# First MLP layer, second product: the low weights of the last F tile multiply all 128 rows

## The chip, the cores and the metric

The program runs on one core of one Trainium2 chip. The metric is device time in microseconds (us), over several executions. The engines are named as in the profile: PE (TensorE, the matmuls), PEld (its weight loads), DVE (VectorE), ACT (ScalarE), POOL (GpSimd), SP (SyncE, which issues most DMAs).

## The reference

Four layers over x of 2048 tokens by 640 channels: a spectral filter, a token MLP, and both again, with residuals. The change lies in the first MLP, whose hidden size F is 1728:

```python
def _B_ref(x, w1, b1, w2, b2):
    h = _layernorm(x, axis=-1)                       # (B, S, D)
    u = jnp.einsum("bsd,sf->bdf", h, w1) + b1        # (B, D, F)
    u = _gelu(u)
    y = jnp.einsum("bdf,fs->bds", u, w2) + b2        # (B, D, S)
    return y.transpose(0, 2, 1)

x = A_x
x = x + _A_ref(_layernorm(x, axis=-1), A_w_r, A_w_i)
x = x + _B_ref(_layernorm(x, axis=-1), B_w1, B_b1, B_w2, B_b2)
x = x + _A_ref(_layernorm(x, axis=-1), A_w_r, A_w_i)
x = x + _B_ref(_layernorm(x, axis=-1), B_w1, B_b1, B_w2, B_b2)
```

## The kernel before

Products in float32 precision are made of 16-bit parts: an operand is split into a high part and a low part (the rest), and three matmuls accumulate high by high, high by low and low by high (`mm3`, line 253). Stationary operands are weights; the moving operand has 320 columns, half of the 640 channels.

The first MLP is `b1st` (line 869). F is cut into 14 tiles of 128 rows (`NFT`). 13 of them are full; the last has 64 rows of its own, and the host lays these 64 out twice, so that rows 64 to 127 of the tile's weights repeat rows 0 to 63. The first product makes u tile by tile. `usplit` (line 918) then splits u: `uh` is the high part, `ul` the low part, one pair of tiles for each F tile. In the last F tile (13) `uh` is written on all 128 rows, then the lower part goes into rows 64 to 127 of `ul`, and rows 0 to 63 of `ul` take a copy of `uh` (lines 919 to 923). Since the weights are there twice, one matmul of the high weights `wh` with this `ul` gives high by high and high by low together. What is left for tile 13 is the low weights `wl` by the high part of u, over the 64 rows 0 to 63.

The second product (loop at line 1033) makes 16 output tiles j of 128 tokens. For each j it runs over the 14 F tiles and, in each, over the halves a = 0 and 1: three matmuls for F tiles 0 to 12 (line 1072), and two for tile 13 (lines 1074 and 1075). Two halves of tile 13 in each of 16 outputs make 32 matmuls of line 1075. In the last j (`tail`) the loop is sorted so that half 0 is done whole before half 1, and the next layer's first transform follows on its tail. Around the matmuls the same loop loads, scans and splits the weights of later outputs (`ahead`, `prep`, `step`), evicts the sum of the output with the bias and the residual x (line 1082), stores it, normalizes the row and folds it for the next layer (line 1086), and, two outputs later, multiplies it by that layer's first table (`flush`, the matmuls written `ps<-tM` in the profile).

PE works its instructions in program order. PSUM tiles come from a ring of four (`big`, line 88). Except in the tail the order on each engine is the order in which a scheduling layer issued the instructions. The helper `Pin` records every operation, so nearly all rows of the profile carry line 48; they are told apart by the names of their tiles.

Of the kernel before, what the change touches and what calls it, by code (L numbers as in the profile page):

```python
# [55 lines left out]
class Layers:  # L56
# [812 lines left out]
    def b1st(self, li):  # L869
        nc, A = self.nc, self.A  # L870
        V, G, T = self.V, self.G, self.T
        mm = self.PE.matmul
# [20 lines left out]
        uh = [pu.tile([128, 2, 320], F16, name=f"uh{f}_{self.n}") for f in range(NFT)]  # L893
# [7 lines left out]
        def ahead(m):  # L901

            if m + 3 < NFT + NJ:
                self.wload(m + 3)
            if m + 1 < NFT + NJ:
                self.wopen(m + 1)

        def prep(m):

            for c in range(2 if m + 1 < NFT + NJ else 0):  # L910
                self.wsplit(m + 1, (c,))
                yield

        def step(m):
            if m in sc:
                next(sc[m])

        def usplit(ft, t):
            V.tensor_scalar(uh[ft], t, self.su, None, op0=ALU.mult)
            c = slice(0 if ft < NFT - 1 else 64, 128)  # L920
            V.scalar_tensor_tensor(ul[ft][c], t[c], self.su[c], uh[ft][c], op0=ALU.mult, op1=ALU.subtract)
            if ft == NFT - 1:
                V.tensor_copy(ul[ft][:64], uh[ft][:64])

        def prod(ps, w, j, h, start=False, stop=False):
            for a in range(2):
                mm(ps[:, a, :320], w[:, j], h[:, a], start=start, stop=stop)
# [20 lines left out]
        for ft in range(NFT):  # L948
# [9 lines left out]
            for j in run:  # L958
                if ft == 0:
                    if j in (6, 7):  # L960
                        step(2)
                elif ft == 1:
                    if j in (1, 2):
                        next(steps)
                    if j in (8, 10):
                        self.scan1(3, (j // 2 - 4,))
                    if j == 15:
                        step(3)
                else:
                    if ft == 2 and j in (4, 5):  # L970
                        step(3)
                    if ft == 2 and j in (5, 6):
                        self.scan1(4, (j - 5,))
                    if ft == 2 and j == 7:
                        step(4)
                    if j in ((6, 8) if ft == 2 else (2, 4)):
                        next(steps)
                    if ft == 2 and j in (10, 11) or ft > 2 and j in (4, 5):
                        step(ft + 2)
                    if j == 8 and ft == NFT - 3:  # L980
                        self.scale_u()
                    if j in (11, 13):
                        self.scan1(ft + 3, (j // 2 - 5,))
                    if j == 15:
                        step(ft + 3)
                    if ft == NFT - 1 and 6 <= j:
                        usplit(j - 6, uf[j - 6])
# [16 lines left out]
        for k in range(10, NFT):  # L1004
            usplit(k, uf[k])
# [11 lines left out]
        def load(j):  # L1017
            if j < NJ - 1:
                xt = self.t(p, [128, D], F32, "xt", 3)
            else:  # L1020
                xt = self.t(p, [128, 642], F32, "zt", 1)
                G.memset(xt[:, D:], 0.0)
            nc.sync.dma_start(xt[:, :D], self.xs[li][j])
            return xt
# [4 lines left out]
        def flush(k):  # L1029
            while len(pend) > k:  # L1030
                self.s1_all(*pend.pop(0))

        for j in range(NJ):
            wh, wl = self.w.pop(NFT + j)
            ahead(NFT + j)
            m = NFT + j
            steps = prep(m)
            c2 = self.ct[1][:, j:j + 1]
            if j + 2 < NJ:
                xts.append(load(j + 2))  # L1040
            xt = xts[j][:, :D]
            T.activation(xt, xt, AF.Identity, bias=self.b2[:, j:j + 1])
            x2 = xt.rearrange("p (a b) -> p a b", a=2)
            tail = j == NJ - 1
            ps = self.big()
            pss = (ps[:, 0], self.big()[:, 0] if tail else ps[:, 1])
            order = [(ft, a) for ft in range(NFT) for a in range(2)]
            if tail:

                order.sort(key=lambda q: q[1])  # L1050
                st = self.t(p, [128, 2, 6], F32, "st", 2)
                self.pin = True

            def half(a):
                V.scalar_tensor_tensor(x2[:, a], pss[a][:, :320], c2, x2[:, a], op0=ALU.mult, op1=ALU.add)
                V.bn_stats(st[:, a], x2[:, a])

            for i, (ft, a) in enumerate(order):
                if tail and i == NFT:
                    half(0)  # L1060
                    flush(1)
                if i in (4, 8):
                    next(steps, None)
                if i in (6, 7):
                    step(m + 2)
                if i in (15, 18):
                    self.scan1(m + 3, (i // 3 - 5,))
                if i == 26 and m + 3 < NFT + NJ:
                    step(m + 3)
                o = pss[a][:, :320]  # L1070
                if ft < NFT - 1:
                    self.mm3(o, (wh[:, ft], wl[:, ft]), (uh[ft][:, a], ul[ft][:, a]), ft == 0, False)
                else:
                    mm(o, wh[:, ft], ul[ft][:, a], start=False, stop=False)
                    mm(o, wl[:64, ft], uh[ft][:64, a], start=False, stop=True)
            if tail:
                half(1)
                nc.sync.dma_start(self.xs[li + 1][j], xt)
                self.a0_tail(j, xts[j], st, pend)
                self.pin = False  # L1080
                break
            V.scalar_tensor_tensor(x2, ps[:, :, :320], c2, x2, op0=ALU.mult, op1=ALU.add)
            nc.sync.dma_start(self.xs[li + 1][j], xt)
            flush(1)
            r, b = self.stats_r(p, *self.stats(p, xt, self.CA, self.CB))
            pend.append((j, *self.a0_lo(*self.a0_hi(self.a0_fold2(self.a0_fold1(self.a0_norm(xt, r, b)))))))
# [616 lines left out]
```

## Time and profile before

| | |
|---|---|
| median of 3 runs | 1053.35 us (1052.02 to 1053.73) |
| span of the profiled execution, first to last instruction | 1049.4 us |
| median less that span | 3.9 us |
| mean granted TensorE clock | 0.976 |
| second product of the first MLP | 371.25 to 568.30 us |
| PE busy from 371.25 to 568.00 | 196.75 of 196.75 us |
| PEld, DVE, ACT, POOL busy in that stretch | 138.73, 120.58, 100.43, 38.72 us |
| DMA, mean share of 16 engines there | 0.39 |

The profile gives one execution; its own total beside the span is not recorded, so the span is compared with the median of the runs. PE and PEld are two rows of the same engine: a weight load can run while the matmul ahead of it runs. A matmul's recorded length (0.30 us) is longer than the step from one matmul to the next, since matmuls are pipelined; what a matmul costs in a full queue is read from the start of one to the start of the next. In matmul rows "128\*128" is contraction rows by output rows, and in "128x320" 320 is the moving columns.

### The profile page before, as it was taken

The numbers are of one execution on the slowest core, as the hardware profiler recorded it, in microseconds if no ns is written. First come the engines' busy times: TensorE is split into PE (matmuls) and PEld (weight loads), VectorE is DVE, ScalarE is ACT, GpSimd is POOL, SyncE is SP. The second block draws the span as 40 slices with busy tenths as digits, with TensorE's granted clock in tenths as the row PEclk, the third lists the DMA queues.
The fourth block names the chain that finished last, engine by engine and source line by source line (L and its number), as shares of the span: only waits on it lengthen the run. The fifth ranks groups of instructions, "written<-read, shape, count | busy, mean of one in ns | idle before, by whom it ended". The sixth has DMA issues, their size and how long they took to land.

```text
span 1049.4 us, 21203 instructions
## 1 busy us (share of the span) xinstructions
PE 1005.2 (96%) x8379; PEld 765.3 (73%) x8379; DVE 750.6 (72%) x1465; ACT 587.2 (56%) x904; POOL 289.2 (28%) x487
## 2 busy tenths in 40 slices
PE   4889898999999999999998998999999999999998
PEld 3768798777777776777775887986777777777776
DVE  7978979954333955666655797997655564987885
ACT  5858668776554555555532575784644454644532
POOL 6938877400000002111121587870000000000000
PEclk8599989999999999999999998999999999999999
DMA  7766355532222264434321652554422233445511
GB/s 230 267 190 201 94 176 198 176 114 89 83 81 78 74 236 152 122 121 134 121 78 55 207 164 98 191 184 165 143 98 82 74 106 94 138 139 178 166 43 51
DMA packets 55739, 141.48 MB, mean 135 GB/s; under 512 B 6460, under 2 KB 12248, under 8 KB 55384
## 3 DMA queue, kind: packets, MB, share of 16 engines
q1 hardware_dynamic: 54200, 131.97, 38.8%
q0 software_dynamic: 1440, 8.15, 2.5%
q8 instruction: 66, 1.08, 0.4%
q14 instruction: 33, 0.27, 0.1%
HBM read 117.03 MB, written 23.07 MB: 134 GB/s over the span
## 4 chain that ended last, share of the span: by engine, by line
PE 78%; DVE 15%; POOL 2%; issue 2%; ACT 1%; DMA 1%; SPq 0%; POOLq 0%; ACTq 0%; DVEq 0%
PE ps L48 78%; DVE xt L48 4%; DVE st L48 2%; DVE el L48 2%; DVE f L48 2%; DVE s1l L48 1%; DVE hl L48 1%; POOL ta L48 1%; DVE xl L48 1%; POOL eo L48 1%; DMA xt<-x 1%; DVE wl L48 0%; DVE ta L48 0%; DVE tb L48 0%; DMA raw<-w 0%
## 5 line engine op out<-in xcount | busy, mean ns | idle before, releaser
L48 PEld LDWEIGHTS <-wh 128*128 128x128 f16 x2992 | 289.5, 98 | 115.0 <-issue 0.8
L48 PEld LDWEIGHTS <-wl 128*128 128x128 f16 (+1 forms) x1616 | 157.8, 98 | 67.8 <-issue 4.5
L48 PE MATMUL ps<-hh,wh 128*128 128x320 f16 x896 | 186.0, 299 | 1.1 <-ACT hh L48 0.6
L48 PE MATMUL ps<-hl,wh 128*128 128x320 f16 x896 | 184.8, 299 | 0.0
L48 PE MATMUL ps<-hh,wl 128*128 128x320 f16 x832 | 171.5, 299 | 0.6 <-DVE wl L48 0.6
L48 DVE SCALAR_TENSOR_TENSOR wl<-raw,s,wh 128x1024 f16<-128x1024 f32 (+2 forms) x88 | 103.6, 1181 | 86.7 <-ACT wh L48 86.7
L48 PE MATMUL ps<-uh,wl 128*128 128x320 f16 x448 | 134.3, 300 | 0.0
L48 PE MATMUL ps<-ul,wh 128*128 128x320 f16 x448 | 133.7, 299 | 0.0
L48 ACT ACTIVATE wh<-raw,s 128x1024 f16<-128x1024 f32 (+2 forms) x92 | 94.8, 1048 | 69.3 <-PE ps L48 63.6
L48 POOL TENSOR_TENSOR r<-v,mh 128x1 f32<-128x1 f32 x64 | 35.5, 555 | 330.4 <-DVE nm L48 323.0
L48 PE MATMUL ps<-uh,wh 128*128 128x320 f16 x416 | 124.4, 299 | 0.0
L48 ACT ACTIVATE junk<-raw 128x896 bf16<-128x896 f32 (+1 forms) x60 | 59.6, 994 | 45.6 <-DMA raw<-w 45.3
L48 PE MATMUL ps<-u,wo 128*128 128x320 f16 x504 | 69.9, 299 | 0.0
L48 DVE TENSOR_TENSOR f<-eo 128x256 f32<-128x256 f32 (+1 forms) x124 | 39.0, 368 | 41.8 <-POOL eo L48 41.2
L48 PEld LDWEIGHTS <-wo 128*128 128x128 f16 x504 | 49.3, 98 | 19.1
L48 PE MATMUL ps<-tDi,yh 128*128 128x322 f32 x256 | 60.2, 322 | 1.2 <-ACT yh L48 1.2
L48 DVE BATCH_NORM_STATS2 st<-xt 128x6 f32<-128x320 f32 x126 | 55.3, 481 | 4.9 <-DMA xt<-x 4.8
L48 ACT ACTIVATE z<-xt,nb,r 128x640 f32<-128x640 f32 x31 | 28.5, 919 | 53.4 <-POOL z L48 42.9
L48 POOL TENSOR_TENSOR eo<-z 128x320 f32<-128x320 f32 x62 | 53.2, 880 | 17.0 <-ACT z L48 15.1
L48 PE MATMUL ps<-ph,tS 128*128 128x321 f16 (+2 forms) x288 | 57.9, 286 | 0.0
L48 PE MATMUL ps<-tM,f 128*128 128x128 f32 x160 | 38.3, 408 | 20.2 <-DMA xt<-x 11.7
L48 PEld LDWEIGHTS ps<-tM,f 128*128 128x128 f32 x160 | 32.3, 290 | 26.1 <-DVE f L48 25.5
(184 smaller groups left out, 2057.2 us busy)
## 6 DMA issues: line engine op xcount, KB each, us to landing
raw<-w SPq DMA_DIRECT2D x56, 512.0 KB
xt<-x SPq DMA_DIRECT2D x79, 320.0 KB
w<-w SPq DMA_DIRECT2D x48, 321.0 KB
x<-xt SPq DMA_DIRECT2D x47, 320.0 KB
raw<-w SPq DMA_DIRECT2D x32, 448.0 KB
raw<-w2z SPq DMA_DIRECT2D x32, 448.0 KB
out<-xt SPq DMA_DIRECT2D x15, 320.0 KB
tIM<-tIM POOLq DMA_DIRECT2D x8, 512.0 KB, 4.8
```

The lines of the kernel that those rows point to most:

```text
L48: i = f(*a, **k)
```

## The change

Two edits in `b1st`. After tile 13 of u is split, POOL writes zeros into rows 64 to 127 of its high part. And the 32 matmuls of the low weights of tile 13 take all 128 rows of the weights and of u instead of rows 0 to 63. The other 64 rows add weights times zero.

```diff
@@ usplit
             V.scalar_tensor_tensor(ul[ft][c], t[c], self.su[c], uh[ft][c], op0=ALU.mult, op1=ALU.subtract)
             if ft == NFT - 1:
                 V.tensor_copy(ul[ft][:64], uh[ft][:64])
+                G.memset(uh[ft][64:], 0.0)
@@ second product, last F tile
                     mm(o, wh[:, ft], ul[ft][:, a], start=False, stop=False)
-                    mm(o, wl[:64, ft], uh[ft][:64, a], start=False, stop=True)
+                    mm(o, wl[:, ft], uh[ft][:, a], start=False, stop=True)
```

The order of the instructions on PE, DVE, ACT and SP stays as it was. POOL has one instruction more, between the last work of the stage ahead of the MLP and the two small zero fills that it issues early for the next layer (`z` and `zt`). Before:

```order
L48 TENSOR_TENSOR r_3324<-v_3320,mh 128x1 [waits DVE_49,Activation_49]
L48 MEMSET z_5410 128x2
L48 MEMSET zt_7343 128x2 [waits PE_49]
L48 TENSOR_TENSOR r_5406<-v_5402,mh 128x1 [waits DVE_49]
L48 TENSOR_TENSOR nb_5408<-nm_5404,r_5406 128x1 [waits DVE_49,Pool_49]
```

With the change, where `uh_610_3417` is tile 13 of the high part and its wait on DVE is for the subtraction that reads these rows:

```order
L48 TENSOR_TENSOR r_3324<-v_3320,mh 128x1 [waits DVE_49,Activation_49]
L48 MEMSET uh_610_3417 64x640 [waits DVE_49,Activation_49,Pool_49]
L48 MEMSET z_5411 128x2 [waits Pool_49]
L48 MEMSET zt_7344 128x2 [waits PE_49]
L48 TENSOR_TENSOR r_5407<-v_5403,mh 128x1 [waits DVE_49]
```

The two small fills now stand behind the fill of `uh`, and the first `r` of the output loop behind these.

On PE, at the end of output j = 0, the rows with the change are these (`wh_5129` and `wl_5130` are the weights of j = 0):

```order
L48 MATMUL ps_5294<-ul_610_3431,wh_5129 128x320 [waits DVE_49]
L48 LDWEIGHTS wl_5130
L48 MATMUL ps_5294<-uh_610_3417,wl_5130 128x320 [waits Pool_49]
L48 LDWEIGHTS wh_5129
L48 MATMUL ps_5294<-ul_610_3431,wh_5129 128x320
L48 LDWEIGHTS wl_5130
L48 MATMUL ps_5294<-uh_610_3417,wl_5130 128x320
```

Before, the same seven rows stood there without the wait on POOL; no later matmul of the loop has gained a wait.

## The prediction

> **What bounds the kernel now.** I read the chain of waits first, then the stage that the change touches, then its matmuls one by one. From the page, the chain that ended last, and the chain cut to the stage:
>
> ```profile
> PE 78%; DVE 15%; POOL 2%; issue 2%; ACT 1%; DMA 1%; SPq 0%; POOLq 0%; ACTq 0%; DVEq 0%
> 359.97 208.33 PE ps L48 x1621
> 568.33 0.56 DVE zt L48
> 571.71 0.73 ACT fht L48
> ```
>
> From 359.97 to 568.3 us the chain never leaves PE. Nothing that another engine does in the second product (371.25 to 568.3) sets the end; what PE saves there, the end saves, until something else becomes late. Behind the product comes a serial tail of DVE and ACT that starts when the last matmul has ended, and so moves with it.
>
> The timeline of PE where output j = 0 passes to j = 1 (start us, length, out<-in, contraction rows by output rows, shape):
>
> ```profile
> 381.32 0.30 PE L48 MATMUL ps<-uh,wl 128*128 128x320 f16 x1
> 381.46 0.30 PE L48 MATMUL ps<-uh,wh 128*128 128x320 f16 x1
> 381.59 0.30 PE L48 MATMUL ps<-ul,wh 128*128 128x320 f16 x1
> 381.73 0.30 PE L48 MATMUL ps<-uh,wl 128*128 128x320 f16 x1
> 381.87 0.30 PE L48 MATMUL ps<-ul,wh 128*128 128x320 f16 x1
> 382.10 0.31 PE L48 MATMUL ps<-uh,wl 64*128 64x320 f16 x1
> 382.33 0.31 PE L48 MATMUL ps<-ul,wh 128*128 128x320 f16 x1
> 382.58 0.31 PE L48 MATMUL ps<-uh,wl 64*128 64x320 f16 x1
> 382.82 0.31 PE L48 MATMUL ps<-uh,wh 128*128 128x320 f16 x1
> ```
>
> The lengths are all alike and PE counts as busy throughout; the starts tell the cost. Four steps among matmuls of 128 rows, 381.32 to 381.87, take 0.55 us, 0.14 each. The four steps into and out of the two matmuls of 64 rows, 381.87 to 382.82, take 0.95 us. The weight loads of the same place say why:
>
> ```profile
> 381.73 0.10 PEld L48 LDWEIGHTS <-wh 128*128 128x128 f16 x1
> 382.09 0.09 PEld L48 LDWEIGHTS <-wl 64*128 64x128 f16 x1 [0.27 <-issue]
> 382.33 0.10 PEld L48 LDWEIGHTS <-wh 128*128 128x128 f16 x1
> 382.57 0.09 PEld L48 LDWEIGHTS <-wl 64*128 64x128 f16 x1
> ```
>
> Among 128-row matmuls a load runs one matmul ahead: the `wh` load of 381.73 ends before the `wh` matmul of 381.87 begins, while the one ahead of it runs. The 64-row load at 382.09 starts only with its own matmul (382.10), after 0.27 us in which the loader waited for nothing that the profile shows, and the 128-row load at 382.33 again only with its own. At each change of height the run-ahead is lost.
>
> Is it the change of height, or the height? Two other places tell:
>
> ```profile
> 582.96 0.23 PE L48 MATMUL ps<-tD,s1l 128*128 128x160 f16 x1
> 583.03 0.23 PE L48 MATMUL ps<-tD,stk 96*128 96x160 f16 x1
> 583.10 0.31 PE L48 MATMUL ps<-tD,s1h 128*128 128x161 f16 x2
> 610.34 0.28 PE L48 MATMUL ps<-tI,xh 64*128 64x128 f16 x4
> 610.51 0.28 PE L48 MATMUL ps<-tI,xh 64*128 64x128 f16 x4
> 610.62 0.22 PE L48 MATMUL ps<-tI,xl 64*128 64x128 f16 x2
> 610.77 0.31 PE L48 MATMUL ps<-ph,tS 128*128 128x321 f16 x1
> ```
>
> A 96-row matmul between 128-row ones steps by 0.07 us on both sides, the same as its neighbours of 160 columns, so fewer rows alone cost nothing. 64-row matmuls among themselves are quick (four of `xh` and two of `xl` between 610.34 and 610.51, 0.03 us each), but the last two and the way out to 128 rows take 0.15 us. The price is on the border between 64 and 128 rows.
>
> **The change, part by part.** The same 32 matmuls with the same 320 columns stay; their count and that of their loads do not change:
>
> ```profile
> L48 PE MATMUL ps<-uh,wl 128*128 128x320 f16 x416 | 124.4, 299 | 0.0
> L48 PE MATMUL ps<-uh,wl 64*128 64x320 f16 x32 | 9.8, 307 | 0.0
> L48 PEld LDWEIGHTS <-wl 64*128 64x128 f16 x32 | 3.0, 93 | 6.7 <-issue 4.5
> 567.75 0.30 PE L48 MATMUL ps<-ul,wh 128*128 128x320 f16 x1
> 567.99 0.31 PE L48 MATMUL ps<-uh,wl 64*128 64x320 f16 x1
> 568.23 0.28 PE L48 MATMUL ps<-tM,fh 128*128 128x128 f16 x2
> ```
>
> Term 1, the borders. Each output has four, and they cost 0.95 - 0.55 = 0.40 us more than four plain steps. The last ones, 0.24 us each at 567.75 to 568.23, cost the same as the first. 16 outputs: 16 x 0.40 = 6.4 us. The very last way out lies behind the matmul that DVE waits for, and PE then stands idle anyhow, so 0.24 - 0.14 = 0.1 us is not gained: 6.3 us. After the change the `uh,wl` matmuls of tile 13 have the form of the 416 others, all steps of which are plain, so I take the whole of it. The 6.7 us that the loader waited ahead of these 32 loads, 0.21 each, is the same loss seen on the loader's side and is not added.
>
> TensorE: Matmul & The Clock Gate, a page of the Trainium skill, says in its section on LDWEIGHTS that a load's time goes by columns and not by contraction rows; by that alone the change would be worth nothing, and it is one of the rivals below. TensorEngine Tiling (Array Packing), of the Trainium skill, says under Key Properties that switching the tiling mode drains TensorE; the border rows above agree. With the first page's drain of about 128 array cycles (Single matmul latency), 53 ns at its 2.4 GHz, 63 borders would give an estimate of 3.4 us; the rows show 0.10 us a border and they decide.
>
> Term 2, the fill and its wait. It is one POOL instruction over 640 columns of 64 rows, released by the subtraction into `ul`:
>
> ```profile
> 380.01 0.89 DVE L48 SCALAR_TENSOR_TENSOR ul<-uf,su,uh 64x640 f16<-64x640 f32 x1
> 380.93 0.32 DVE L48 COPY ul<-uh 64x640 f16<-64x640 f16 x1
> 393.67 0.55 POOL L48 TENSOR_TENSOR r<-v,mh 128x1 f32<-128x1 f32 x1 [194.16 <-DVE nm L48]
> L48 POOL MEMSET z<- 128x2 f32 x31 | 3.0, 98 | 0.0
> L48 POOL TENSOR_TENSOR yl<-Y,yh 128x512 fp32r<-128x512 f32 x30 | 44.0, 1466 | 7.9 <-ACT yh L48 7.9
> L48 POOL COPY xl<-xl 128x126 f16<-128x126 f16 x30 | 8.6, 287 | 1.8 <-DVE xl L48 1.8
> ```
>
> No fill of this size stands in the trace. From below, a fill of two columns takes 0.10 us; from above, a subtraction of 512 columns, which reads two operands, takes 1.47, or 1.8 for 640. I take 0.8, halfway between the two-column fill and a copy of f16 scaled by columns (0.287 x 640 / 126 = 1.5), since a fill reads nothing. It starts at 380.90, when the subtraction ends, and is done at 381.7 (381.0 to 382.7). PE asks for it at the first `uh,wl` of tile 13, which without the border comes at 381.87 + 0.14 = 382.0. So the wait is nothing by my value and 0.7 us at worst, once; later outputs find the zeros there. Below nothing is excluded: the fill removes no work. All of PE is queued behind that matmul, so a wait there is paid in full. Behind the fill on POOL stand two small fills and then the `r` of 393.67, 11 us later; POOL stood idle for 194 us before that one, so it is hidden. Should the fill hold up the DVE copy beside it, the copy ends at 381.25 and is wanted at 381.87: 0.6 us of cover.
>
> Term 3, what a faster PE could run into. Weights and sums must be ready 0.4 us earlier for each output. The tightest place that I find is the first eviction, which waits for its residual row:
>
> ```profile
> 390.49 2.48 ACT L48 ACTIVATE xt<-xt,b2s 128x640 f32<-128x640 f32 x3 [5.83 <-DMA xt<-x]
> 391.35 0.88 DVE L48 SCALAR_TENSOR_TENSOR xt<-ps,c,xt 128x640 f32<-128x640 f32 x1 [4.30 <-ACT xt L48]
> ```
>
> It frees the sum of j = 0 at 392.23. By the ring of four (one tile for each product, one for each scale) j = 2 takes that tile. j = 1 has 82 matmuls from 382.82 on: 78 plain steps of 0.55 / 4 and the four of 0.95 are 11.7 us, so j = 2 starts near 394.5, and 2 x 0.4 earlier, near 393.7, with the change. 1.5 us of cover is left even if the row of x comes no earlier, and nothing is charged. Without cover the price would be what the row of x is late, once, since the later rows are loaded two outputs ahead.
>
> Sum: -6.3 + 0 + 0. The profiled span of 1049.4 us becomes 1043.1. The median of the runs lies 3.9 us above that span; with the same around it, 1053.35 - 6.3 = 1047.0 us, 0.6% less.
>
> **The clock.** One thing can move either way. Behind the product PE has little to do, and then the granted clock (the column after POOL, in stretches of the span) falls to half:
>
> ```profile
> 569.30:573.30 4.00, 0.31 (x3) 0.14 (x4) 3.35 (x13) 1.69 (x3) 1.08 (x2) 1.00 0.55 166
> 573.30:580.20 6.90, 6.26 (x48) 5.67 (x49) 2.30 (x5) 1.28 (x4) 0.00 (x0) 0.51 0.59 207
> ```
>
> PE was busy for 0.31 of 4.0 us and then had a clock of 0.51 for 6.9 us. Such a stretch costs up to half of itself, 3.4 us. The idle stretch after the product comes 6.3 us earlier with the change; whether the clock falls after it again I can't read from one execution. I expect it as before, and keep 3.4 us on both sides.
>
> **The rivals.**
> (a) The forecast, borders gone: 1047.0.
> (b) One low-clock stretch less, 1043.6, or one more, 1050.4. For it: the stretch follows an idle gap of a few us, and other gaps of the span could bring one or lose it. Against: the gap that brings one here keeps its length.
> (c) Half of the border price stays, because a load also waits where the accumulation of a half ends and not only for the height: 1053.35 - 3.2 = 1050.2. For it: all 64-row matmuls of this stage end an accumulation. Against: the steps in cost the same as the steps out, and only the steps out stand behind an end.
> (d) Nothing is gained, 1053.3: the loss would belong to tile 13's place in the program and not to its rows. Against it are the 96-row rows and the way out at 610.62.
> (e) Slower: the wait on POOL is long. Its place is the first `uh,wl` of tile 13 in j = 0; each us that the fill ends after 382.0 costs one us. It decides from 6.3 us on, a fill of 7.4 us (380.90 to 388.3); at 12 us, the end at 392.9, it would be 1047.0 + 10.9 = 1057.9. For it: the size is not in the trace. Against: POOL's subtraction of 512 columns has a mean of 1.47 us, and `r`, one column, took 0.55 us after 194 us of idling, so waking costs POOL no more than that.
>
> **How the numbers follow.** (a) 0.80; (b) 0.09, of which 0.04 for less and 0.05 for more; (c) 0.04; (d) 0.04; (e) 0.03. This kernel's measurement can tell about 0.2%, 2.1 us, from no change. (a), (b) and (c) are faster by more: 0.93. (d) is the same: 0.04. (e) is slower: 0.03. The range goes from one clock stretch less, 1043.6, to one more, 1050.4, which also holds the 0.7 us of wait and (c); about 0.07 lies outside.
>
> **What would show it.** Right: between 370 and 560 us the 32 `uh,wl` matmuls of tile 13 step by 0.14 us, their loads run one matmul ahead, the 0.27 us issue wait is gone, and the last matmul of the product starts near 561.7 instead of 567.99 if the part ahead is unchanged; the fill ends before 382.0; PE has no idle time in the product. Wrong: steps of 0.23 at these places ((c), (d)), a PE wait on POOL near 382 ((e)), a PE wait on DVE `xt` near 394, or a different number of half-clock stretches (b).

## The result and the profile after

| | before | with the change |
|---|---|---|
| median, 6 runs each | 1053.16 us | 1049.95 us |
| ratio, 95% interval | | 0.9968 [0.9958, 0.9979] |
| the same kernel once more, 5 runs (before: 11) | 1052.48 us | 1047.94 us, 0.9959 [0.9947, 0.9971] |
| span of the profiled execution | 1049.4 us | 1047.3 us |

The kernel became 0.3 to 0.4% faster, 3 to 4.5 us, where 6.3 were forecast. The border that was forecast is gone. The timeline of PE at the end of output j = 0 in the changed kernel, and that of its loader:

```profile
382.96 0.30 PE L48 MATMUL ps<-ul,wh 128*128 128x320 f16 x1
383.09 0.30 PE L48 MATMUL ps<-uh,wl 128*128 128x320 f16 x1
383.23 0.30 PE L48 MATMUL ps<-ul,wh 128*128 128x320 f16 x1
383.39 0.30 PE L48 MATMUL ps<-uh,wl 128*128 128x320 f16 x1
383.52 0.30 PE L48 MATMUL ps<-ul,wh 128*128 128x320 f16 x1
383.66 0.30 PE L48 MATMUL ps<-uh,wl 128*128 128x320 f16 x1
383.79 0.30 PE L48 MATMUL ps<-uh,wh 128*128 128x320 f16 x1
```

```profile
383.09 0.10 PEld L48 LDWEIGHTS <-wh 128*128 128x128 f16 x1
383.23 0.10 PEld L48 LDWEIGHTS <-wl 128*128 128x128 f16 x1
383.39 0.10 PEld L48 LDWEIGHTS <-wh 128*128 128x128 f16 x1
383.52 0.10 PEld L48 LDWEIGHTS <-wl 128*128 128x128 f16 x1
```

The four steps from 383.23 to 383.79 take 0.56 us, where they took 0.95, and every load runs one matmul ahead. From its first to its last matmul the product takes 190.18 us (372.61 to 562.78) after 196.74 (371.25 to 567.99): 6.6 us less. But the chain that ended last, a line of the page, has changed its face:

```profile
PE 58%; DVE 22%; ACT 7%; DMA 5%; POOL 5%; issue 3%; SPq 0%; POOLq 0%; ACTq 0%; DVEq 0%
```

PE held 78% of it before. A third of that is given back right behind the product. The first matmul of the last row's transform (`fht`) and the second eviction of that row (`zt`) in the two kernels, before:

```profile
568.33 0.55 DVE L48 SCALAR_TENSOR_TENSOR zt<-ps,c,zt 128x320 f32<-128x320 f32 x1 [2.17 <-PE ps L48]
572.49 0.28 PE L48 MATMUL ps<-tM,fht 128*128 128x128 f16 x2 [3.25 <-ACT fht L48]
```

and with the change:

```profile
562.78 0.30 PE L48 MATMUL ps<-uh,wl 128*128 128x320 f16 x1
565.32 0.54 DVE L48 SCALAR_TENSOR_TENSOR zt<-ps,c,zt 128x320 f32<-128x320 f32 x1
569.47 0.40 PE L48 MATMUL ps<-tM,fht 128*128 128x128 f16 x2 [4.83 <-ACT fht L48]
```

Before, DVE had waited 2.17 us for PE when the last matmul ended. Now PE has ended at 563.1 and DVE comes to the eviction 2.2 us later, without a wait: DVE is late. From the last matmul to `fht` it is 6.69 us in place of 4.50, and PE idles for 4.83 there in place of 3.25. By parts of the two profiled executions: product -6.57, tail (from the last matmul to `fht`) +2.18, the stages behind +0.95, the start ahead of the product, which the change does not touch, +1.36; the sum is the -2.07 of the spans.

Why DVE is late is read from the evictions of the outputs (`xt<-ps,c,xt`). Two of them before, and the last two:

```profile
434.19 0.88 DVE L48 SCALAR_TENSOR_TENSOR xt<-ps,c,xt 128x640 f32<-128x640 f32 x1
446.33 0.88 DVE L48 SCALAR_TENSOR_TENSOR xt<-ps,c,xt 128x640 f32<-128x640 f32 x1
542.70 0.88 DVE L48 SCALAR_TENSOR_TENSOR xt<-ps,c,xt 128x640 f32<-128x640 f32 x1 [0.39 <-PE ps L48]
555.10 0.88 DVE L48 SCALAR_TENSOR_TENSOR xt<-ps,c,xt 128x640 f32<-128x640 f32 x1 [1.19 <-PE ps L48]
```

The same outputs (j = 4, 5, 13, 14) with the change:

```profile
435.23 0.88 DVE L48 SCALAR_TENSOR_TENSOR xt<-ps,c,xt 128x640 f32<-128x640 f32 x1
447.37 0.88 DVE L48 SCALAR_TENSOR_TENSOR xt<-ps,c,xt 128x640 f32<-128x640 f32 x1
543.27 0.88 DVE L48 SCALAR_TENSOR_TENSOR xt<-ps,c,xt 128x640 f32<-128x640 f32 x1
554.36 0.88 DVE L48 SCALAR_TENSOR_TENSOR xt<-ps,c,xt 128x640 f32<-128x640 f32 x1
```

In both kernels the evictions come 12.14 us apart in the middle of the product; they do not follow PE, they follow each other. PE needs 12.42 us for an output before and 12.00 with the change. Call the time from the end of an output's last matmul to its eviction the lag. Before, it is 8.5 us at j = 0, where the row of x comes late, and 3.9 at j = 1, since the second eviction follows after 7.03 us; from j = 2 on the evictions catch up by 0.28 us an output, and they wait for PE at the end. With the change they fall behind by 0.14 an output: the lag is 4.9 us at j = 4, 5.9 at j = 11 and 4.1 at j = 14 (549.97 + 0.31 to 554.36). After j = 11 it shrinks, where the loop has no later weights left to scan: the last scan starts at 519.06, and the last of these evictions come 11.20 and 11.09 us apart. The chain of waits of the changed kernel, cut to one such period, shows what the 12.14 us are made of (rows of 0.2 us and less left out; "issue" is time in which the engine waited for nothing that the profile shows):

```profile
495.81 0.72 ACT xt L48
496.53 0.94 ACT wh L48
...
497.49 1.15 DVE wl L48
498.64 0.80 DVE st L48 x2
499.44 0.72 DVE s1l L48
...
500.28 1.01 DVE wl L48
...
502.30 0.92 ACT z L48
...
503.29 1.70 POOL eo L48 x2
...
505.01 1.04 DVE f L48 x4
...
506.41 0.51 issue
506.92 1.03 ACT junk L48 x2
507.95 0.72 ACT xt L48
```

A ring over ACT, DVE and POOL: the row's statistics, normalization and folds, with the scan (`junk`) and the split (`wh`, `wl`) of later weights queued in between, and then the next row. No engine in it is near full (DVE 62%, ACT 52%, POOL 21% of the product), and the ring is full. In five other periods the chain goes from `z` to `junk` through the load of a later row of x in place of `eo` and `f`: `z` also frees the buffer of that load, which lands 3.2 to 3.4 us later (at 433.70, say, before the `junk` of 434.09). These periods are 12.14 us long as well; the two ways are nearly equal, so a shorter `eo` or `f` alone might gain a few tenths at most. That was not tried.

### The profile page after: what moved, and what is told of

Read it like the earlier page. It is cut to its first block, busy times and chain, and to the rows that moved or that the text cites. A ratio compares the mean times of both kernels' runs of the same rounds, so it can differ in the third digit from the quotient of the medians.

```text
span 1047.3 us, 21205 instructions
## 1 busy us (share of the span) xinstructions
PE 1001.3 (96%) x8379; PEld 769.2 (73%) x8379; DVE 751.5 (72%) x1465; ACT 586.3 (56%) x904; POOL 289.0 (28%) x488
## 4 chain that ended last, share of the span: by engine, by line
PE 58%; DVE 22%; ACT 7%; DMA 5%; POOL 5%; issue 3%; SPq 0%; POOLq 0%; ACTq 0%; DVEq 0%
PE ps L48 58%; DVE xt L48 5%; DVE wl L48 3%; DVE st L48 3%; DMA xt<-x 3%; POOL eo L48 3%; DVE f L48 2%; DVE s1l L48 2%; DVE el L48 2%; ACT z L48 1%; ACT wh L48 1%; ACT junk L48 1%; DVE hl L48 1%; ACT xt L48 1%; DMA w<-w 1%
## 5 line engine op out<-in xcount | busy, mean ns | idle before, releaser
L48 PEld LDWEIGHTS <-wl 128*128 128x128 f16 x1616 | 157.9, 98 | 62.4 <-DVE wl L48 0.9
L48 PE MATMUL ps<-tM,f 128*128 128x128 f32 x160 | 40.6, 437 | 19.0 <-DVE f L48 19.0
L48 PEld LDWEIGHTS ps<-tM,f 128*128 128x128 f32 x160 | 35.4, 319 | 23.9 <-DVE f L48 23.5
```

The source lines that it names most:

```text
L48: i = f(*a, **k)
```

## The experiments

All times are medians of device time; the ratio is to runs of before on the same chip. Product: from the first to the last matmul start of the second product; tail: from there to the first `fht` matmul; both from the timeline of PE.

| run | us | ratio to before, 95% | product | tail |
|---|---|---|---|---|
| after_again | 1047.94 | 0.9959 [0.9947, 0.9971] | 190.15 | 7.09 |
| low_pairs | 1048.10 | 0.9966 [0.9954, 0.9978] | 193.60 | 4.50 |
| rows_early | 1047.16 | 0.9950 [0.9938, 0.9962] | 191.89 | 4.50 |
| x_first | 1046.09 | 0.9945 [0.9933, 0.9957] | 190.15 | 4.50 |
| fill_alone | 1052.75 | 0.9997 [0.9988, 1.0005] | 196.74 | 4.50 |
| before_x_first | 1052.54 | 1.0004 [0.9994, 1.0014] | 196.74 | 4.50 |
| longer_row | 1057.55 | 1.0042 [1.0027, 1.0058] | 196.81 | 8.77 |
| x_first_rows_early | 1044.71 | 0.9918 [0.9905, 0.9932] | 190.15 | 4.50 |
| x_first_2 | 1046.14 | 0.9938 [0.9925, 0.9952] | 190.15 | 4.50 |
| both_2 | 1045.33 | 0.9932 [0.9918, 0.9947] | 190.15 | 4.50 |

**The changed kernel once more.**

> The changed kernel once more, beside the three others on one chip, so that they can be compared with it: 3.2 us below before, near 1050. In its profile the product lasts 190.2 us from its first to its last matmul and the step from there to the first matmul of the last row's transform 6.7 us, if the row chain causes the loss; if the loss is one of the clock alone, that step varies with the clock stretches.

The median fell further than expected, by 4.5 us and not 3.2, with overlapping intervals. The product is the same to 0.03 us, and the tail is again long. It is longer than the first time by 0.40 us (7.09 after 6.69), and so is the lag of the eviction of row 14 (4.48 after 4.08): tail and lag go together.

**The border, priced by halving its number.** Before, with the two 64-row matmuls of an output side by side:

```diff
-                    mm(o, wl[:64, ft], uh[ft][:64, a], start=False, stop=True)
+                    for b in (a,) if tail else (0, 1) if a else ():
+                        mm(pss[b][:, :320], wl[:64, ft], uh[ft][:64, b], start=False, stop=True)
```

> Before, with the two 64-row matmuls of an output put side by side (both high ones, then both low ones) in the first 15 outputs: two borders an output in place of four. Theory (the border between 64 and 128 rows costs 0.10 us): 15 x 2 x 0.10 = 3.0 us less in the product. Its period of 12.22 us stays above the 12.14 of the row chain, so the lag of the evictions falls by 0.08 a row, is below 1 us at row 14, and the tail loses nothing: 1053.2 - 3.0 = 1050.2. Rival (each 64-row matmul costs 0.20 us, wherever it stands): nothing gained, 1053.2.

The product fell by 196.74 - 193.60 = 3.14 us for 30 borders taken away, 0.105 us each; the rival is out. By the medians it is 4.4 us, more than the 3.0 expected, but the interval, 2.3 to 4.8 us, holds both: with half of the borders left, this kernel is as fast as the changed one, since its tail loses nothing. The timelines of PE and of its loader at the end of j = 0:

```profile
381.71 0.43 PE L48 MATMUL ps<-ul,wh 128*128 128x320 f16 x2
382.08 0.44 PE L48 MATMUL ps<-uh,wl 64*128 64x320 f16 x2
382.45 0.31 PE L48 MATMUL ps<-uh,wh 128*128 128x320 f16 x1
```

```profile
382.07 0.11 PEld L48 LDWEIGHTS <-wl 64*128 64x128 f16 x2 [0.27 <-issue]
382.45 0.11 PEld L48 LDWEIGHTS <-wh 128*128 128x128 f16 x2 [0.26 <-issue]
```

Two waits of the loader are left for each pair, one on the way in and one on the way out. The tail stayed at 4.50, though for another reason than expected: the scheduler laid the row work differently here. The second scan of an output stands on ACT ahead of `fh`, where ACT had been waiting for DVE, and no longer between `fh` and the `xt` behind it; the evictions came 11.45 us apart, not 12.14, and had caught up by j = 9.

**The row chain, made shorter.** The changed kernel with the normalization and folds of row j moved into output j + 1, behind the split of the weights, its statistics ahead of it, and the order pinned from j = 2 on:

```diff
+            self.pin = j >= 2
...
+                if i == 9:
+                    fold1()
+                if i == (13 if tail else 20):
+                    fold2()
...
-            flush(1)
             r, b = self.stats_r(p, *self.stats(p, xt, self.CA, self.CB))
-            pend.append((j, *self.a0_lo(*self.a0_hi(self.a0_fold2(self.a0_fold1(self.a0_norm(xt, r, b)))))))
+            flush(1)
+            late.append((j, xt, r, b))
```

Here `fold1` is the normalization and the first fold of the row in `late`, `fold2` the second fold and its split.

> The changed kernel with the row work (statistics, normalization, folds) of output j ahead of the weight splits of output j+1, in a pinned order from j = 2 on. Theory (row chain): its period falls from 12.14 us to about 9 us, well below the 12.00 of the product; the evictions catch up, row 14 is evicted when its product ends, and the 2.2 us of the tail come back: 1050.0 - 2.2 = 1047.8, with 4.5 us from the last matmul to the first of the last row's transform. Rival (the loss lies in the granted clock): 1050, and the tail as it falls. Should the new order bring a PE wait on the low weights, it is slower.

The evictions waited for PE from j = 4 on, and the tail is back at 4.50. One wait of PE came in, where the late first rows meet the pinned order; it is the only one of the product:

```profile
409.85 0.16 PE L48 MATMUL ps<-sqb,ones 128*128 128x1 bf16 x1 [1.57 <-DVE sqb L48]
```

It eats most of the 2.2 us, as the product of 191.89 in place of 190.15 shows. The median of 1047.16 lies 0.8 us below that of the changed kernel in the same set of runs, where 2.2 were expected, and the intervals overlap; the parts of the profile decide here, not the time.

**The row chain, started earlier.** The changed kernel with the first two rows of x loaded ahead of most of the next layer's tables:

```diff
-        for q in range(4):
-            self.a0_load_m(q)
-        self.a0_load()
...
         xts = [load(0), load(1)]
+        for q in range(4):
+            self.a0_load_m(q)
+        self.a0_load()
         pend = []
```

> The changed kernel with the first two rows of x loaded ahead of the next layer's tables. Theory (row chain): the first eviction no longer comes 8.4 us late; from near 0 the lag grows by 0.14 us a row to about 1.5 us and is gone by row 14, so the tail loses nothing: 1047.8, 2.2 below the changed kernel. If the tables hold up something else, less. Rival (clock): 1050.

The evictions still come 12.14 us apart, but they start 2.6 us behind PE and not 8.4, and stand 0.65 behind at j = 14. The second eviction of the last row waits for PE again, and the tail is 4.50:

```profile
562.17 0.30 PE L48 MATMUL ps<-uh,wl 128*128 128x320 f16 x1
562.51 0.55 DVE L48 SCALAR_TENSOR_TENSOR zt<-ps,c,zt 128x320 f32<-128x320 f32 x1 [1.16 <-PE ps L48]
566.67 0.28 PE L48 MATMUL ps<-tM,fht 128*128 128x128 f16 x2 [3.36 <-ACT fht L48]
```

1046.09 against 1047.94 us of the changed kernel in the same set of runs: 1.85 us, of 2.2 expected. The intervals of the two ratios overlap, so here too the tail of the profile carries the proof. The page's chain again has PE at 78%.

**The same two edits without the change.**

> Before, with the first two rows of x loaded ahead of the next layer's tables and the 64-row matmuls kept. Theory (row chain): with the product at 12.42 us an output the chain of 12.14 us catches up by itself, the tail of 4.5 us waits for PE alone, and nothing is gained: 1052.5. Rival: the earlier loads are worth 1.8 us by themselves, as between the changed kernel and x_first: 1050.6.

Nothing is gained (1.0004). The earlier x is worth something only once PE has become faster than the row chain.

**The fill alone.**

> Before, with the zero fill alone: rows 64 to 127 of the high part are filled, the 64-row matmuls stay and do not read them. Theory: the fill (0.77 us on POOL in the changed kernel) is hidden, so 1052.5, as before, and the product 196.7 us. Rival: the fill holds something up, 0.5 to 1 us more.

Nothing is lost. In the changed kernel the fill was near to its price and nearer to a wait than I thought:

```profile
382.56 0.77 POOL L48 MEMSET uh<- 64x640 f16 x1 [181.77 <-DVE ul L48]
```

It ends at 383.33, and the first `uh,wl` of tile 13 starts at 383.39, after a step of 0.16 us in place of 0.14. In the second run of the changed kernel the fill ended 0.27 us ahead of that matmul, and the step was 0.14.

**The row chain, made longer.** The changed kernel with one copy more on ACT for each row:

```diff
             T.activation(xt, xt, AF.Identity, bias=self.b2[:, j:j + 1])
+            T.activation(xt, xt, AF.Copy)
```

> The changed kernel with one more copy in place of the row of x on ACT for each output (0.73 us, the result is the same). Theory (row chain): the chain's period goes from 12.14 to 12.87 us, the lag grows by 0.87 us a row, and 14 rows come about 10 us later at the tail: 1048 + 10 = 1058. Rival (PE bounds the product and ACT, busy half the time, has room): 1048.

9.6 us slower than the changed kernel on the other chip, as the chain says and as no count of busy time would: the evictions came 12.92 us apart. Most of it did not show up in the tail (8.77 us), though, but inside the product, which took 6.7 us more than in the changed kernel. When the lag had grown to 9.2 us, the first matmul of an output began to wait for a free one of the four sum tiles, which `s1l`, the split of an earlier row's transform, had to read out first. The waits of PE from 373 to 570 us, 5.3 of the 6.7:

```profile
PE ps L48 <- DVE s1l L48: 4.5, 6, 0.9
PE ps L48 <- DVE fl L48: 0.6, 1, 0.6
PE ps L48 <- ACT fh L48: 0.2, 1, 0.2
```

**Both edits.**

> The changed kernel with both the earlier x and the earlier row work. Theory: with either alone the tail is back at 4.50 us, so both together gain nothing over x_first: 1046.1, if the one PE wait of 1.6 us that rows_early had on the sum for the scale goes with the late first rows, and 1047.7 if it stays. Rival (the chain still costs something in x_first): 1045 or less.

Product and tail are those of x_first, the PE wait is gone, and yet the median was 1.4 us lower, on another chip. So the two were run side by side:

> x_first once more, beside the version with both edits: on two chips the two gave 0.9945 and 0.9918 of before, though product and tail are equal in their profiles (190.15 and 4.50 us). If the profiles hold the whole effect, the two are equal on one chip within 1 us, near 1046 to 1047.

> Both edits once more. Equal to x_first_2 within 1 us if product and tail hold the whole effect; 1.4 us or more below it if earlier row work gains something that the two parts do not show.

They agree within 0.8 us, and the intervals overlap almost wholly. Both are the fastest versions tried, 0.6 to 0.8% under before; which of them is better is left open.

## Why the prediction was right about the border and too large in its sum

**The border** was right: its place, its cause and its size. 6.3 us were forecast for the product and 6.57 measured; the small rest is that I read the steps from rounded starts. Rivals (c) and (d), that the place or the end of the accumulation costs, fell with the changed kernel itself, where the same places and ends have plain steps, and low_pairs ties the cost to the number of borders. TensorEngine Tiling (Array Packing), of the Trainium skill, has the rule under Key Properties that a change of tiling mode drains TensorE. Low_pairs agrees in that each border has its price, but no run here shows a drain as such; the 53 ns that I had estimated from the other page of the Trainium skill is half of the 0.105 us measured.

**The fill** was right: 0.77 us where I took 0.8, hidden. The cover of 0.3 us that I forecast was used up in the first run of the changed kernel and was 0.27 in the second.

**Term 3 failed.** "The tightest place that I find is the first eviction", and past it "nothing is charged". I looked for the places where PE would have to wait for something inside the product, found 1.5 us of cover at the first, and stopped. The runs showed that the loss needs no PE wait: the rows are evicted in a ring of their own, one each 12.14 us, with sums piling up in the ring of four. At 12.42 us an output PE was slower than that ring; at 12.00 it is faster, and the difference is paid when PE has ended and the last row is not yet through. Its size was there to be read. In the profile before, the evictions waited for PE three times, 0.39, 1.19 and 2.17 us; these 3.75 us are all the room that the rows had against PE. By this estimate 2.5 of the 6.3 us forecast could not reach the end (2.8 of the 6.57 measured); the tail lost 2.2 and 2.6 in the two runs. The first sentence of the prediction, that "what PE saves there, the end saves, until something else becomes late", held, but I asked what would be late for PE and not what would be late behind it. The chain that I started from, PE alone from 359.97 to 568.33, names what ended last; it does not tell how little room the next one had. That 1049.95 still lies under the upper end of the range, 1050.4, is luck: that end was made for a longer half clock and for half of the border price, and the loss of the tail is neither.

**The clock**, my rival (b), did not make the tail long: DVE is late there, and rows_early has the longer half clock with the short tail. Rival (b) came in part all the same. The gap that it starts in did not keep its length (4.83 us after 3.25), and in both runs of the changed kernel the half clock behind the product lasted 10.2 us, not 6.8. What that cost is not settled: from `fht` to the next MLP the changed kernel took 132.8 and 132.4 us and rows_early 133.0, where before took 132.05, but longer_row, with 10.2 us of half clock too, took 131.7. The wait of rival (e) did not come.

With the measured parts the sum reads -6.6 for the product and +2.2 for the tail: -4.4, or 1049. The measured 1049.95 and 1047.94 lie around it.

## What to carry to other kernels

When the bounding engine gets faster, work out the period of every ring of the other engines that it runs beside, not only whether they are busy: take two occurrences of the same instruction in the middle of the stage and compare their distance with that of the bounding engine. A ring that catches up by 2% an iteration falls behind after a gain of 3%, and the bill comes at the end of the stage or when the buffers are full. And a matmul of 64 rows alone among matmuls of 128 was dearer here than one of 128 with zeros (0.24 against 0.14 us); look at starts, since the lengths and the busy share hide it.

## What was not expected of the hardware

Executions with the same instructions up to there reach the second product's first matmul at different times: 371.25 us in before, 372.61 and 370.55 in two runs of the changed kernel, 373.84 in fill_alone. That is a spread of 3.3 us, about the size of the gain. The traces' clock records name a candidate: ahead of the product the half clock lasted 30.7 us in the run that came at 370.55, 37.5 in before, and 41.0 in the two that came at 372.61 and 373.84. Equal stretches still differ by 1.2 us, so it is not the whole cause, and no run tests it. A single pair of profiled spans (here 2.1 us apart) therefore said less than the parts of the stage: the product repeated to 0.03 us, the tail to 0.40.
